# The order of big and small tiles in an expert layer behind an FFT, on one core

## The chip, the core and the metric

The kernel runs on one core of a Trainium2 chip. The metric is device microseconds (us) of one execution. Engines: TensorE (PE, its weight loads PEld), VectorE (DVE), ScalarE (ACT), GpSimd (POOL) and SyncE (SP, which issues most DMA transfers).

## What is computed

```
X = fft(fft(x, axis=1), axis=2).real          # x: 8 x 3072 x 256, so 24576 rows of 256
h = X @ w_in;  g = h * clip(h + 3, 0, 6) / 6;  y = g @ w_out         # first MoE, d_ff 2048
e = argmax(y @ w_gate);  p = softmax(y @ w_gate)[e]                  # 8 experts
out[row] = p * (relu(y @ w1[e]) @ w2[e])                             # second MoE, d_ff 1024
```

## The kernel before

The transform and the first MoE run first, in steps, and scatter each routed row into a region of its expert in DRAM (`xs`). The change does not touch them. Then comes the second MoE, which works in **tiles** of rows of one expert: 41 **big** ones (`NBIG`) of 512 rows, which their experts fill, and 21 **small** ones (`NSMALL`) of 256 rows for what remains; the last three small ones (`SPARE`) run only if the counts need them, and did not here. So 59 tiles run. Tiles 0 and 1 are started early, beside the first MoE. The table of experts and first rows of the others is worked out on the chip in `regs`, big ones first; SP loads an entry of it for each DMA address.

I call the position of a tile in the order of work its **place**, 0 to 58. For the tile at place `i`, `tile_of(i)` writes down:

- `first(i)`: for each of 8 blocks `f` of d_ff, 6 matmuls into one of four PSUM banks (`hp`); ACT takes the high part out (`WA`, relu), DVE the low part (`WB`, a scalar_tensor_tensor, "the low part of hidden block f" below). A bank is free again when DVE has done its low part.
- `prep_w(i + 1)` and `prep_x(i + 1)`: the next tile's weights and rows are split into high and low parts. For weights ACT copies the high part and POOL subtracts (`w1` in two halves, `w2` in two pieces); `prep_w`'s argument sends the first half of `w1` to DVE in some cases. For rows there are, in this order: ACT and DVE each put one 16-bit half of each word into `xf` (ACT an activation, DVE a COPY), ACT copies the high part `xT`, DVE subtracts (`xT <- xf, xT`, "the x subtract" below), and DVE makes the places for the output scatter (`dst`; a CAST for a big tile, two operations on `inv` for a small one).
- `load_x(i + 2)` and `load_w(i + 2)`: DMA from SP's queue, two places ahead. The weights of a tile are 2 MB whatever its rows.
- `second(i)`: for each 128 rows, 24 matmuls (three for each block f, the third of them with the low part) into `op`; DVE scales into `yo`, POOL scatters to `out`.

Buffers alternate with the place: an odd place works from `TB`, `W2a`/`SC`, `xTb`, and during it the next place's `xTa` is made; an even place works from `W1b`, `W2b`, `xTa`, and `xTb` is made. A scheduler fixes the order on each engine before the run, and each engine then takes its instructions strictly in that order, so an instruction is often ahead of where the text has it: `w2` of place i + 1 is split at the start of place i, and `w1` of place i + 2 in the middle of it.

Of the kernel before, what the change touches and what calls it, by code (L numbers as in the profile page):

```python
# [17 lines left out]
ALU = mybir.AluOpType  # L18
AX = mybir.AxisListType
PSUM = bass.MemoryType.PSUM  # L20
SP_ONLY = [mybir.EngineType.SP]

P = 128
# [4 lines left out]
XW = 260  # L28
# rows of a big tile, which its expert fills, and of a small one, which takes what remains
TBIG, TS = 512, 256  # L30
CAPR = NTOK + TS
NBIG = -(-(NTOK - NE * (TBIG - 1)) // TBIG)
NSMALL = (NTOK - NBIG * TBIG + NE * (TS - 1)) // TS
# the tiles that start before the first MoE ends, of the expert with the most rows by then
NEARLY = 2
# [5 lines left out]
SPARE = 3  # L41
# [22 lines left out]
HW = 3 * 4 * 129  # L64
# kind, parity, first column, range of d
X_SEG = ((0, 0, X_T0, 0, 129), (0, 1, X_T1, 1, 128), (1, 0, X_T2, 0, 129), (2, 1, X_T2 + 128, 1, 128),
         (2, 0, X_T3, 0, 129), (1, 1, X_T3 + 128, 1, 128))

# The transform over the sequence splits by s = 1024 a + 3 b (mod 3072) into one over a (3 points) and one
# over b (1024 points) without factors between them; the one over d is merged into w_in. A row k and its  # L70
# mirror -k share the parts P (even in d) and Q (odd in d): h_k = A - B, h_-k = A + B, with A = P W', B = Q W'.


@with_exitstack
def tile_fft_moe(ctx, tc, xr, xf, xcoef, w_in, w_out, w_gate, w1, w2, tabs, fm, misc, tri, sgn8, dstc, maskc, out):
# [16 lines left out]
    est = pa.tile([P, NE], F32, name="est")  # L92
    # what the second MoE uses again
    WA = [pa.tile([P, DFF], F32R, name=f"WA{i}") for i in range(2)]
    WB = [pa.tile([P, DFF], F32R, name=f"WB{i}") for i in range(2)]
    TB = pa.tile([P, 2, 2, TW], F32R, name="TB")
    SC1 = pa.tile([P, 2, 2, 2, 256], F32R, name="SC1")
    # places that hold one tile after another: SS0, SS1, HH0, HH1, RR, pq (two)
    pr = ctx.enter_context(tc.tile_pool(name="pr", bufs=1))
# [54 lines left out]

    # a bank of PSUM for small things
    def bank(name):
# [31 lines left out]

    # ---------------------------------------------------------------- folds of x
    def fold_quarter(R, H, hf, e1, e2):  # L190
# [12 lines left out]

    # kind 0 first: the group g = 0 needs no other
    def fold_whole(H):
# [20 lines left out]

    # closures for one batch: loads and folds of the two half tiles in order, and the splits of each half tile
    def fold_ops(b, e1, e2, rtiles=None):
# [21 lines left out]

    # ---------------------------------------------------------------- transform over b
    PASS = ((0, 0), (0, 1), (1, 0))
# [74 lines left out]

    # the part of d = 128, row 0 of Q, on all partitions
    def fft_bc(b, g, pq):
# [10 lines left out]

    # a group's transform: list of (mm, ev) pieces, and its tiles
    def fft_group(b, g):
# [4 lines left out]

    # ---------------------------------------------------------------- start: constants
    def load_consts():
# [29 lines left out]

    # the folds of the rows b = 256 and 768, which the halves leave out, for all batches: [kind, parity, columns, place]  # L380
    def start_x256():
# [17 lines left out]

    # float64 comes as int64. Times 2^-112, its high word, read as float32, leaves 5 bits of exponent, so that a shift  # L400
    # by 3 makes room for the next bits of the fraction and gives float32; what float32 can't hold goes to 0
    def conv(raw, hi, lo):
# [33 lines left out]

    # w_in's chunk of two blocks of columns: to parts in a half of SC1, which the stacks fill later; then times the transform
    def w_in_conv(c):
# [25 lines left out]

    # logits straight from g: w_out times w_gate beside w_out
    def w_out_mm(c):
# [13 lines left out]

    # ---------------------------------------------------------------- first MoE
    def mm1(ab, f0, pq, c0):
# [16 lines left out]

    # one tile for the rows k of a step, one for their mirrors  # L500
    def halves(tag, dt, s):
# [28 lines left out]

    # a row's high halves of its words, then its low halves
    def halve(xo, xp):
# [4 lines left out]

    # routing of nt token tiles, first of number t0; closures in stages
    def routing(xo, xp, t0, nt, mask, tagn, wait=RKW):
# [64 lines left out]
    if True:  # L604
# [91 lines left out]

        # the folds of batch b + 1 beside batch b, on steps without transforms and ranks
        def plan_folds(b):
# [34 lines left out]

        # the rows of k = 1536 of each batch
        def plan_extra(base):
# [61 lines left out]

        # ------------------------------------------------------------ second MoE: its tiles
        T = {}
# [11 lines left out]

        # what the second early tile waits for
        def second_set():
# [3 lines left out]
        hh = [[W.rearrange("p (f n) -> p f n", n=TBIG) for W in Ws] for Ws in (WA, WB)]  # L817

        def rows(i):
            return TBIG if i < NBIG else TS  # L820

# [9 lines left out]
        def load_x(i):  # L831
            t = T[i] = {}
            n = rows(i)
            v = er[0:1, i:i + 1] if i < NEARLY else regs[0:1, 0, i - NEARLY:i - NEARLY + 1]
            r = ds(reg(v, NE * CAPR - n), n)
            t["gd"] = pk.tile([P, 4, 2], F32, tag="gd", name=f"gd{i}")[:, 0:n // P]
            sp.dma_start(t["gd"], xs.bitcast(F32)[r, D:D + 2].rearrange("(t p) c -> p t c", p=P))
            for w in range(2):
                for k in range(2):
                    c = w * D + k * P  # L840
                    sp.dma_start(xset(i)["x"][:, w, k, 0:n], xs16[r, c:c + P], transpose=True)

        def load_w(i):
            s = kset(i)
            e = reg(er[0:1, 2:3] if i < NEARLY else regs[0:1, 1, i - NEARLY:i - NEARLY + 1], NE - 1)
            sp.dma_start(s["w1"], w1[ds(e, 1)].rearrange("e (k p) f -> p (e k) f", p=P))
            for f0, f1, t in s["w2"]:
                sp.dma_start(t.rearrange("p (f d) -> p f d", d=D),
                             w2[ds(e, 1), f0 * P:f1 * P].rearrange("e (k p) d -> p (e k) d", p=P))

        # closures: the parts of a tile's weights
        def prep_w(i, eng):
# [11 lines left out]
        def prep_x(i):  # L864
            t, v = T[i], xset(i)
            n = rows(i)
            nt = n // P
            xf, t["xT"] = v["xf"][:, :, 0:n], [z[:, :, 0:n] for z in v["xT"]]
            h = xf.bitcast(U16).rearrange("p k (n w) -> p k n w", w=2)
            keep = tc.keep_in_program_order  # L870
            keep(act.activation(h[:, :, :, 1], v["x"][:, 0, :, 0:n], AF.Copy))
            keep(dve.tensor_copy(h[:, :, :, 0], v["x"][:, 1, :, 0:n]))
            act.activation(t["xT"][0], xf, AF.Copy)
            sub(dve, t["xT"][1], xf, t["xT"][0])
            t["dst"] = pk.tile([P, 4], I32, tag="dst", name=f"dst{i}")[:, 0:nt]
            if i < NBIG:
                keep(dve.tensor_copy(t["dst"], t["gd"][:, :, 1]))
            else:
                inv = pk.tile([P, 2], F32, tag="inv", name=f"inv{i}")
                keep(dve.tensor_scalar(inv, iot, vld[:, i - NBIG:i - NBIG + 1], BIG, op0=ALU.is_lt, op1=ALU.mult))  # L880
                keep(dve.tensor_tensor(out=t["dst"], in0=inv, in1=t["gd"][:, :, 1], op=ALU.add))

        # the early tiles' expert and places, from the counts so far
        def early_mm():
# [108 lines left out]

        # ------------------------------------------------------------ the list of tiles
        cps = bank("cps")
# [14 lines left out]

        # per tile: its expert, and its number among the expert's
        def spread(i0, n):
# [16 lines left out]
        dve.tensor_tensor(out=nf[:, 1:NE], in0=cum[:, 1:NE], in1=cum[:, 0:NE - 1], op=ALU.subtract)  # L1029
        # per tile: the sum over its expert of what v holds per expert  # L1030
        def pick(r, v, o, sh):
# [28 lines left out]

        # ------------------------------------------------------------ second MoE
        pd = ctx.enter_context(tc.tile_pool(name="pd", bufs=1, reuse_waits="tile"))
# [21 lines left out]
        def tile_of(i):  # L1084
            if i:
                first(i)
            if i + 1 < last and i:
                if i + 1 >= NEARLY:
                    for f in prep_w(i + 1, lambda n: pool if n or i + 1 < NBIG else dve):
                        f()  # L1090
                prep_x(i + 1)
            if i and i + 2 < last:
                load_x(i + 2)
                load_w(i + 2)
            second(i)
# [19 lines left out]

# [1 line left out]
def _round12(a):  # L1117
# [73 lines left out]

# how the 12 parts (a, row, side) of a batch go into each segment, for its row of high and its row of low parts
def _xcoef():
# [69 lines left out]
```

## Time and profile before

| what | us |
|---|---|
| median of 3 runs (3367.33 to 3371.47) | 3368.87 |
| span of the profiled execution | 3376.2 |
| PE busy in that span | 3082.8 (91%) |
| DVE busy | 2691.3 (80%) |
| POOL busy | 2296.7 (68%) |
| ACT busy | 1809.4 (54%) |
| second MoE from the first matmul of place 1 to the end of the span | 1189.0 |

The page gives no other duration for the profiled execution than its span, which is 7.3 us (0.2%) longer than the median of the timed runs. Shares are means over the whole span; the second MoE is its last third.

### The profile page before, as it was taken

What the parts mean: (1) busy time and instruction counts of PE and PEld (TensorE: products, weight loads), DVE (VectorE), ACT (ScalarE), POOL (GpSimd) and SP (SyncE); (2) the same over time, 40 slices, a digit from 0 to 9 for tenths busy, and PEclk for the clock granted to TensorE, in tenths of its full rate; (3) what the DMA queues carried; (4) which work ended last, traced back from release to release, by engine and by line L of the source; (5) the groups of instructions that cost most, each with busy time, mean ns of one, the idle gap of its engine ahead of it and who ended that gap; (6) DMA issues with size and microseconds to landing.
All of it is one profiled execution on the core that took longest, in us unless ns stands there. A gap on an engine that the chain in (4) does not pass through costs nothing.

```text
span 3376.2 us, 61155 instructions
## 1 busy us (share of the span) xinstructions
PE 3082.8 (91%) x22698; PEld 2948.4 (87%) x22698; DVE 2691.3 (80%) x4453; ACT 1809.4 (54%) x2971; POOL 2296.7 (68%) x1780
## 2 busy tenths in 40 slices
PE   6888889889899989989989999999999999999887
PEld 5888889888899888888988999888899899988787
DVE  8999999999999999999999998845455444546775
ACT  4555555556555555556556665545444544444553
POOL 5576776876866876876876665576666666665654
PEclk8999999999999999999999999999999999999998
DMA  5100100100100100100000001174544454444562
GB/s 188 42 34 23 42 23 14 39 23 14 42 25 14 42 25 14 42 25 14 33 15 15 14 14 51 44 196 140 150 135 137 141 150 133 136 143 133 171 166 74
DMA packets 246975, 242.79 MB, mean 72 GB/s; under 512 B 148523, under 2 KB 209804, under 8 KB 246672
## 3 DMA queue, kind: packets, MB, share of 16 engines
q1 hardware_dynamic: 225424, 184.35, 18.9%
q0 software_dynamic: 21248, 54.48, 4.4%
q8 instruction: 181, 2.97, 0.4%
q14 instruction: 122, 1.00, 0.1%
HBM read 159.71 MB, written 54.04 MB: 63 GB/s over the span
## 4 chain that ended last, share of the span: by engine, by line
PE 45%; DVE 40%; issue 6%; ACT 5%; POOL 2%; DMA 1%; SPq 0%; ACTq 0%; DVEq 0%; POOLq 0%
PE op L163 16%; DVE r L505 15%; PE hp L163 14%; PE acc L510 7%; DVE S L187 7%; PE ab L163 6%; DVE h L182 4%; DVE h L179 4%; ACT r L498 2%; POOL gl L182 1%; DVE H L179 1%; DVE SC L176 1%; DVE H L187 1%; DVE R L179 1%; ACT gh L944 1%
## 5 line engine op out<-in xcount | busy, mean ns | idle before, releaser
L182 POOL TENSOR_TENSOR gl<-r,gh 128x512 fp32r<-128x512 f32 x768 | 1134.3, 1500 | 491.1 <-ACT gh L944 271.4
L510 PE MATMUL acc<-WO,gh 128*128 128x264 f32 x6144 | 844.5, 291 | 15.0 <-ACT xo L529 12.6
L510 PEld LDWEIGHTS acc<-WO,gh 128*128 128x128 f32 x6144 | 805.8, 196 | 16.7 <-ACT xo L529 13.0
L944 ACT ACTIVATE gh<-r 128x512 fp32r<-128x512 f32 x768 | 474.7, 630 | 573.5 <-DVE r L505 437.5
L505 DVE SCALAR_TENSOR_TENSOR r<-r,h 128x512 f32<-128x512 f32 x768 | 733.7, 980 | 36.9 <-ACT r L498 35.8
L498 ACT ACTIVATE r<-h,half 128x512 f32<-128x512 f32 x768 | 523.3, 720 | 236.2 <-DVE h L182 170.7
L163 PE MATMUL ab<-pq,WA 128*128 128x256 f32 x2304 | 425.7, 295 | 155.9 <-DVE rt_mc L548 67.3
L978 DVE SCALAR_TENSOR_TENSOR WB<-hp,WA 128x512 fp32r<-128x512 f32 (+1 forms) x472 | 280.8, 607 | 296.5 <-ACT WA L977 291.0
L163 PEld LDWEIGHTS ab<-pq,WA 128*128 128x128 f32 x2304 | 343.2, 197 | 168.7 <-issue 142.3
L510 PE MATMUL acc<-WO,gl 128*128 128x264 f32 x3072 | 441.2, 285 | 4.8 <-POOL gl L182 4.6
L163 PE MATMUL ab<-pq,WB 128*128 128x256 f32 x2304 | 419.7, 292 | 0.0
L510 PEld LDWEIGHTS acc<-WO,gl 128*128 128x128 f32 x3072 | 402.6, 189 | 7.3 <-POOL gl L182 7.3
L187 DVE SCALAR_TENSOR_TENSOR S<-pb,w,ab 128x256 f32<-128x256 f32 x768 | 334.7, 471 | 55.1 <-PE ab L163 53.5
L977 ACT ACTIVATE WA<-hp 128x512 fp32r<-128x512 f32 (+1 forms) x472 | 245.1, 528 | 214.8 <-PE hp L163 210.0
L163 PEld LDWEIGHTS ab<-pq,WB 128*128 128x128 f32 x2304 | 346.5, 199 | 0.0
L147 POOL DMA_INDIRECT out_dram<-yo,dst x200 | 228.3, 1141 | 147.8 <-DVE yo L1078 121.1
L163 PE MATMUL hp<-xTa,W1b 128*128 128x512 f32 (+1 forms) x1392 | 284.7, 362 | 22.5 <-DVE WB L978 22.5
L163 PEld LDWEIGHTS hp<-xTa,W1b 128*128 128x128 f32 x1392 | 232.4, 189 | 67.4 <-DVE WB L978 25.0
L163 PE MATMUL hp<-xTb,TB 128*128 128x512 f32 (+1 forms) x1344 | 273.9, 363 | 14.8 <-DVE WB L978 14.8
L163 PE MATMUL op<-W2b,WA 128*128 128x256 f32 x1568 | 286.4, 285 | 0.0
L163 PEld LDWEIGHTS hp<-xTb,TB 128*128 128x128 f32 x1344 | 225.6, 192 | 55.8 <-DVE WB L978 16.1
L147 POOL DMA_INDIRECT xs_dram<-xp,pic x192 | 211.3, 1100 | 84.1 <-issue 36.9
(267 smaller groups left out, 5174.8 us busy)
## 6 DMA issues: line engine op xcount, KB each, us to landing
w1a<-in_w_dram SPq DMA_DIRECT2D x29, 1024.0 KB, 5.6
w1b<-in_w_dram SPq DMA_DIRECT2D x29, 1024.0 KB, 5.6
w2b<-in_w_dram SPq DMA_DIRECT2D x58, 512.0 KB, 3.4
R<-in_xr_dram SPq DMA_DIRECT2D x32, 774.0 KB, 4.1
w2a<-in_w_dram SPq DMA_DIRECT2D x29, 768.0 KB, 4.8
w2d<-in_w_dram SPq DMA_DIRECT2D x28, 256.0 KB, 4.3
raw<-in_w_in_dram SPq DMA_DIRECT2D x8, 512.0 KB, 3.8
rawo<-in_w_out_dram SPq DMA_DIRECT2D x8, 512.0 KB, 3.3
```

Of the source, the lines that this page charges most:

```text
L147: i = pool.indirect_dma_start(oob_is_err=False, **kw)
L163: pe.matmul(dst, l, r, start=(n == 0), stop=(n == len(terms) - 1))
L176: pinned(dve.scalar_tensor_tensor(out=lo, in0=src, scalar=scale, in1=hi, op0=ALU.mult, op1=ALU.subtract))
L179: pinned(eng.tensor_tensor(out=o, in0=a, in1=b, op=ALU.add))
L182: i = eng.tensor_tensor(out=o, in0=a, in1=b, op=ALU.subtract)
L187: pinned(dve.scalar_tensor_tensor(out=o, in0=a, scalar=s, in1=b, op0=ALU.mult, op1=ALU.add))
L498: act.activation(r, h, AF.Relu, bias=half, scale=1.0 / 6.0)
L505: dve.scalar_tensor_tensor(out=g, in0=r, scalar=1.0, in1=h, op0=ALU.min, op1=ALU.mult)
L510: pe.matmul(acc[t][:, 0:GW], lhs, wo(w, f0 + i), start=st, stop=sp_)
L944: act.activation(gh[n], g[n], AF.Copy)
L977: act.activation(hi, ps, AF.Relu)
L978: dve.scalar_tensor_tensor(out=lo, in0=ps, scalar=0.0, in1=hi, op0=ALU.max, op1=ALU.subtract)
```

## The change

Before, place and tile number are the same: big tiles at places 0 to 40, small ones at 41 to 58. The change adds a list `order` from place to tile: after the two early tiles come two or three big tiles to each small one, so that the 18 small ones that run stand at places 4, 7, 10, 13, 16, 20, 23, 26, 29, 32, 35, 39, 42, 45, 48, 51, 54 and 58. `rows`, the table lookups and the test for a small tile go through the list. In `tile_of` the rule for the first half of `w1` changes: it goes to DVE when the *current* tile is small, where it went to DVE when the *next* one was small. Buffers, sizes and the number of tiles stay. The rest of the diff deletes comments.

```
+        order = list(range(NEARLY))
+        nb, ns = NBIG - NEARLY, NSMALL - SPARE
+        for n in range(ns):
+            order += range(NEARLY + n * nb // ns, NEARLY + (n + 1) * nb // ns)
+            order.append(NBIG + n)
+        order += range(NBIG + ns, NBIG + NSMALL)
+
         def rows(i):
-            return TBIG if i < NBIG else TS
+            return TBIG if order[i] < NBIG else TS
...
-            v = er[0:1, i:i + 1] if i < NEARLY else regs[0:1, 0, i - NEARLY:i - NEARLY + 1]
+            o = order[i] - NEARLY
+            v = er[0:1, i:i + 1] if i < NEARLY else regs[0:1, 0, o:o + 1]
...
-            if i < NBIG:
+            if order[i] < NBIG:
                 keep(dve.tensor_copy(t["dst"], t["gd"][:, :, 1]))
...
-                    for f in prep_w(i + 1, lambda n: pool if n or i + 1 < NBIG else dve):
+                    for f in prep_w(i + 1, lambda n: pool if n or rows(i) == TBIG else dve):
```

How instructions move is seen at three places. Names carry a running number at their end; line numbers of the changed kernel are 10 higher (L978 has become L988, L182 is the same helper), and `hp_0` to `hp_7` are a tile's eight hidden blocks.

On DVE, within the first products of a small tile at an odd place; before, place 41:

```order
L978 SCALAR_TENSOR_TENSOR WB_71<-hp_0_36603,WA_69 128x256
L978 SCALAR_TENSOR_TENSOR WB_71<-hp_1_36612,WA_69 128x256
L182 TENSOR_TENSOR xTa_26321<-xfa,xTa_26320 128x2x256
L978 SCALAR_TENSOR_TENSOR WB_71<-hp_2_36621,WA_69 128x256
L978 SCALAR_TENSOR_TENSOR WB_71<-hp_3_36630,WA_69 128x256
L978 SCALAR_TENSOR_TENSOR WB_72<-hp_4_36639,WA_70 128x256
```

and after, place 23:

```order
L988 SCALAR_TENSOR_TENSOR WB_71<-hp_0_32343,WA_69 128x256
L988 SCALAR_TENSOR_TENSOR WB_71<-hp_1_32352,WA_69 128x256
L988 SCALAR_TENSOR_TENSOR WB_71<-hp_2_32361,WA_69 128x256
L182 TENSOR_TENSOR xTa_26321<-xfa,xTa_26320 128x1024
L988 SCALAR_TENSOR_TENSOR WB_71<-hp_3_32370,WA_69 128x256
L988 SCALAR_TENSOR_TENSOR WB_72<-hp_4_32379,WA_70 128x256
```

The x subtract has twice the columns, since the next tile is big, and stands one block later.

On DVE, within the first products of a small tile at an even place; before, place 42:

```order
L978 SCALAR_TENSOR_TENSOR WB_71<-hp_2_36783,WA_69 128x256
L182 TENSOR_TENSOR xTb_27748<-xfb,xTb_27747 128x2x256
L978 SCALAR_TENSOR_TENSOR WB_71<-hp_3_36792,WA_69 128x256
L978 SCALAR_TENSOR_TENSOR WB_72<-hp_4_36801,WA_70 128x256
L880 TENSOR_SCALAR inv_36850<-iot,vld 128x2
L978 SCALAR_TENSOR_TENSOR WB_72<-hp_5_36810,WA_70 128x256
L881 TENSOR_TENSOR dst_36849<-inv_36850,gd_36694 128x2
L978 SCALAR_TENSOR_TENSOR WB_72<-hp_6_36819,WA_70 128x256
L182 TENSOR_TENSOR W1b_27742<-w1b,W1b_27741 128x1024
L978 SCALAR_TENSOR_TENSOR WB_72<-hp_7_36828,WA_70 128x256
L872 COPY xfa<-xa 128x2x256
```

and after, place 20:

```order
L988 SCALAR_TENSOR_TENSOR WB_71<-hp_3_31772,WA_69 128x256
L182 TENSOR_TENSOR xTb_27748<-xfb,xTb_27747 128x1024
L988 SCALAR_TENSOR_TENSOR WB_72<-hp_4_31781,WA_70 128x256
L988 SCALAR_TENSOR_TENSOR WB_72<-hp_5_31790,WA_70 128x256
L988 SCALAR_TENSOR_TENSOR WB_72<-hp_6_31799,WA_70 128x256
L887 CAST dst_31829<-gd_31616 128x4
L988 SCALAR_TENSOR_TENSOR WB_72<-hp_7_31808,WA_70 128x256
L1088 TENSOR_SCALAR yo_31846<-op_0_31847,gd_31396 128x256
```

The x subtract now stands behind the fourth low part, the half of `W1b` and the COPY are gone from here, and a CAST stands ahead of the last low part.

On POOL, in the same two tiles; before, place 42:

```order
L147 DMA out_dram<-yo_36706,dst_36467 24576x256 x2
L182 TENSOR_TENSOR SC_74<-w2a,W2a_26317 128x1536
L182 TENSOR_TENSOR SC_74<-w2d,W2a_26317 128x512
L182 TENSOR_TENSOR W1b_27742<-w1b,W1b_27741 128x1024
L147 DMA out_dram<-yo_36868,dst_36687 24576x256
```

and after, place 20:

```order
L147 DMA out_dram<-yo_31628,dst_31391 24576x256 x4
L182 TENSOR_TENSOR SC_74<-w2a,W2a_26317 128x1536
L182 TENSOR_TENSOR SC_74<-w2d,W2a_26317 128x512
L182 TENSOR_TENSOR W1b_27742<-w1b,W1b_27741 128x1024 x2
L147 DMA out_dram<-yo_31846,dst_31609 24576x256
L182 TENSOR_TENSOR W2b_27744<-w2b,W2b_27743 128x1024
L147 DMA out_dram<-yo_31846,dst_31609 24576x256
```

Both halves of `W1b` are POOL's in a small tile now; the half that DVE does has moved into the big tile ahead of it.

## Rows read from the trace of the kernel before

**Rows 1.** Windows (length, engines' busy us, PEclk, DMA share, GB/s): places 1-39, 41-57, 58.

```profile
2187.20:3069.40 882.20, 880.31 (x5618) 794.11 (x5617) 444.32 (x597) 421.09 (x549) 582.37 (x316) 1.00 0.51 147
...
3093.10:3352.40 259.30, 215.83 (x1635) 212.16 (x1634) 185.32 (x253) 128.50 (x235) 153.91 (x84) 0.92 0.51 148
3352.40:3376.20 23.80, 11.47 (x97) 11.26 (x96) 4.85 (x11) 3.09 (x8) 2.92 (x3) 0.81 0.06 19
```

**Rows 2.** Windows of one small tile each: places 41, 42 and 57.

```profile
3093.10:3108.70 15.60, 13.14 (x98) 12.93 (x97) 11.17 (x15) 7.08 (x14) 9.13 (x5) 0.89 0.35 108
3108.70:3122.90 14.20, 11.74 (x99) 11.53 (x98) 11.23 (x15) 8.28 (x15) 8.41 (x5) 1.00 0.55 164
...
3336.90:3352.40 15.50, 13.07 (x99) 12.87 (x98) 7.74 (x13) 4.85 (x11) 6.78 (x4) 0.89 0.06 22
```

**Rows 3.** Waits from 3093.1 to 3352.4: total, times, longest (us).

```profile
PE hp L163 <- DVE WB L978: 34.7, 14, 2.6
...
PE op L163 <- DVE WB L978: 8.8, 3, 2.9
```

**Rows 4.** Groups by form, 3093.1 to 3352.4: busy us, mean ns, idle before.

```profile
L978 DVE SCALAR_TENSOR_TENSOR WB<-hp,WA 128x256 fp32r<-128x256 f32 x136 | 53.9, 416 | 29.6 <-ACT WA L977 26.1 <-ACT W2a L859 3.5
L182 DVE TENSOR_TENSOR xTb<-xfb,xTb 128x512 fp32r<-128x512 f32 x8 | 29.4, 3672 | 0.8
...
L182 POOL TENSOR_TENSOR W1b<-w1b,W1b 128x1024 fp32r<-128x1024 f32 x8 | 19.1, 2391 | 31.0 <-ACT W1b L859 31.0
...
L859 ACT ACTIVATE W1b<-w1b 128x1024 fp32r<-128x1024 f32 x16 | 16.9, 1054 | 21.1 <-PE hp L163 21.1
```

**Rows 5.** Timeline, place 41 (from 3093.1): start, us, engine, instruction [idle before].

```profile
3094.57 0.79 ACT L871 ACTIVATE xfa<-xa 128x512 uint16<-128x512 uint16 x1
...
3096.13 3.45 DVE L182 TENSOR_TENSOR xTa<-xfa,xTa 128x512 fp32r<-128x512 f32 x1
3099.51 0.74 DVE L978 SCALAR_TENSOR_TENSOR WB<-hp,WA 128x256 fp32r<-128x256 f32 x2
...
3096.65 2.38 POOL L182 TENSOR_TENSOR W2b<-w2b,W2b 128x1024 fp32r<-128x1024 f32 x1
...
3099.97 0.39 PE L163 MATMUL hp<-xTb,TB 128*128 128x256 f32 x1 [2.46 <-DVE WB L978]
```

**Rows 6.** Timeline, place 42 (from 3108.7).

```profile
3109.64 0.61 ACT L859 ACTIVATE W2a<-w2d 128x512 fp32r<-128x512 f32 x1
...
3110.66 3.52 POOL L182 TENSOR_TENSOR SC<-w2a,W2a 128x1536 fp32r<-128x1536 f32 x1
3114.12 1.28 POOL L182 TENSOR_TENSOR SC<-w2d,W2a 128x512 fp32r<-128x512 f32 x1
...
3112.26 3.70 DVE L182 TENSOR_TENSOR xTb<-xfb,xTb 128x512 fp32r<-128x512 f32 x1
...
3116.34 0.86 PE L163 MATMUL hp<-xTa,W1b 128*128 128x256 f32 x5 [2.46 <-DVE WB L978]
```

**Rows 7.** Timeline, big tiles at places 35 (from 2956.6) and 36.

```profile
2968.31 5.30 POOL L182 TENSOR_TENSOR TB<-w1a,TB 128x1024 fp32r<-128x1024 f32 x2 [5.70 <-ACT TB L859]
...
2969.36 2.02 DVE L872 COPY xfa<-xa 128x1024 uint16<-128x1024 uint16 x1
...
2971.47 1.06 ACT L873 ACTIVATE xTa<-xfa 128x1024 fp32r<-128x1024 f32 x1 [1.81 <-DVE xfa L872]
...
2972.57 2.13 DVE L182 TENSOR_TENSOR xTa<-xfa,xTa 128x1024 fp32r<-128x1024 f32 x1 [0.82 <-ACT xTa L873]
...
2980.60 1.36 ACT L871 ACTIVATE xfb<-xb 128x1024 uint16<-128x1024 uint16 x1
```

**Rows 8.** Timeline near 2142, beside the first MoE.

```profile
2142.85 1.25 DVE L877 CAST dst<-gd 128x4 int32<-128x4 f32 x1
...
2138.84 6.49 POOL L182 TENSOR_TENSOR gl<-r,gh 128x512 fp32r<-128x512 f32 x4
```

**Rows 9.** Timeline, PE at place 40, the last big tile.

```profile
3077.38 2.84 PE L163 MATMUL hp<-xTa,W1b 128*128 128x512 f32 x11 [0.78 <-DVE WB L978]
```

More of the change, by code (lines that the diff above doesn't have):

```diff
@@ L844, in load_w @@
             s = kset(i)
-            e = reg(er[0:1, 2:3] if i < NEARLY else regs[0:1, 1, i - NEARLY:i - NEARLY + 1], NE - 1)
+            o = order[i] - NEARLY
+            e = reg(er[0:1, 2:3] if i < NEARLY else regs[0:1, 1, o:o + 1], NE - 1)
             sp.dma_start(s["w1"], w1[ds(e, 1)].rearrange("e (k p) f -> p (e k) f", p=P))
@@ L879, in prep_x @@
                 inv = pk.tile([P, 2], F32, tag="inv", name=f"inv{i}")
-                keep(dve.tensor_scalar(inv, iot, vld[:, i - NBIG:i - NBIG + 1], BIG, op0=ALU.is_lt, op1=ALU.mult))
+                keep(dve.tensor_scalar(inv, iot, vld[:, order[i] - NBIG:order[i] - NBIG + 1], BIG, op0=ALU.is_lt, op1=ALU.mult))
                 keep(dve.tensor_tensor(out=t["dst"], in0=inv, in1=t["gd"][:, :, 1], op=ALU.add))
```

## The prediction

> **What bounds the kernel now.** I read the windows first, cut at the first matmul of a place. Places 1 to 39, all big, take 882.2 us with PE busy for 880.3 at a granted clock of 1.00 [rows 1]: 22.62 us each, and nothing on another engine or a queue shows. In units of 256 columns a big tile is 192 matmuls, so one takes 0.118 us, a hidden block of a small tile (6 of them) 0.707, its first product 5.65 and the whole small tile 11.31. The 17 small tiles at places 41 to 57 take 259.3 us, 15.25 each: 3.94 more than PE needs, 67.0 us in all. That is the most that the change can win.
>
> Next I asked what PE waits for there: 17 waits of 43.5 us together, all for a low part on DVE [rows 3]. The rest is mostly clock. Place 42 takes 14.2 us at 1.00, place 41 takes 15.6 at a mean of 0.89 [rows 2], so part of it ran at the lower level, 1.2 GHz of 2.4, and that costs 1.4 us; 11 of the 17 windows, the first and the last among them, are under 1.00.
>
> Why is DVE late? At place 41 the x subtract starts at 3096.13 and takes 3.45 us, while POOL subtracts `W2b` from 3096.65 to 3099.03 [rows 5]; it ends 0.55 after POOL does. At place 42 it waits likewise for two subtracts of POOL, `SC` from `w2a` and from `w2d`, to 3115.40, and ends at 3115.96 [rows 6]. So it can't run beside a POOL subtract. The low parts queued behind it come late, and so do the PSUM banks: at place 41 block 6 is due 4.24 us into the tile and starts at 6.87; at place 42 block 7 is due at 4.95 and starts at 7.64. Delays of 2.6 and 2.7; with some 0.2 to fill the pipeline this gives 11.31 + 2.69 + 0.2 = 14.2, as measured.
>
> **What moves.** A small tile's two neighbours are now big. Averages would say that its weights, x and DMA then have 22.6 us of cover, and DVE, ACT and POOL are all less than full there. But the question is what stands in the 11.3 us of the small tile itself, in order. I take the times of the rows and put the new order under them; t is the time from the tile's first matmul.
>
> *Odd places, eight small tiles (7 to 51).* POOL's second `W2b` subtract keeps its place, t = 3.55 to 5.93 [rows 5]: a big tile ahead is followed by the same scatter, as at place 41. ACT's first x half starts at 1.47 [rows 5], takes 1.36 for 1024 columns in place of 0.79, then come two high parts and the copy of 1.06 [rows 7], so the x subtract is ready at 4.4, after POOL has begun. It ends 1.09 behind POOL's end (2974.70 against 2973.61 for the same form in a big tile [rows 7]): at 7.02. Behind it stands the fourth low part, 0.42 [rows 4], done at 7.4; block 7 needs its bank at 4.95. Delay 2.5, hardly less than now. A tile takes 11.31 + 2.5 + 0.2 = 14.0, and with the lower clock as often as now (11/17 of 1.4 = 0.9) 14.9; eight take 119.3.
>
> *Even places, nine small tiles (4 to 54).* ACT is free of `W2a` at 1.55 [rows 6]; two high parts, the x half (1.36), two high parts and the copy (1.06) make the x subtract ready at 4.9. Four low parts stand ahead of it, done by 4.4, so no bank is late. POOL is in its `SC` pair until t = 6.70 [rows 6], the subtract ends at 7.79 and the fifth low part at 8.2. The second product, from 5.65, needs it for its 15th matmul at 7.30: 0.9 late. Then comes a new collision. POOL now does both halves of `W1b` here, the first when ACT has copied it (6.6, from 1.05 behind block 7's third matmul) and the port is free: 7.75 to 10.2 at 2.39 to 2.45 each [rows 4, 7]. DVE comes to the CAST at 8.7. A CAST of the same 4 columns took 1.25 us beside POOL's subtracts [rows 8], so it too waits; here until 10.2. The last low part, behind it, is done at 10.65, and the 24th matmul wanted it at 8.36: delay 2.3 in all, the 0.9 included. That is 13.8 us a tile. The stall is in two parts of 0.9 and 1.4 with matmuls between, so I give it half the clock loss, 0.45: 14.25, and 128.3 for nine.
>
> *The rest.* The 17 take 247.6 in place of 259.3: 11.7 less. Place 40 loses its wait of 0.8 [rows 9]. Place 58 is small and last as before, without an x subtract ahead of it. The DVE half of `w1` (1.2 us) stands in the big tile ahead of a small one, between its last two low parts; a big tile has four banks of 1.41 us ahead and its second product wants the last low part only 2.6 us after it starts, so I cost this at nothing; with a stall of 1 us at each of 17 it would take the gain back. SP's queue has the same loads, two places ahead, behind the same releases; DMA is busy for 0.51 in both stretches [rows 1], no PE wait ends at a transfer, and a tile ahead of or behind a small one has more time than small ones have now. Sum: 12.5 us less, 3363.7 for the profiled span of 3376.2, which is 7.3 over the median; from the median, **3356**.
>
> **A rule weighed.** The subtract at place 42 was issued before POOL's second `SC` subtract began and still let it pass: it ends 0.56 behind that one [rows 6], and the eight of this kind in the stretch take 3.67 on average [rows 4]. At place 35 the COPY that came during POOL's first `TB` subtract ended at 2971.38, before the second one did at 2973.61 [rows 7]. So the port goes over between two POOL instructions in one case and not in the other. The Trainium skill, "SBUF — State Buffer", section "Who interferes with whom", says that of a DVE operation with two SBUF inputs and a GpSimd operation reading SBUF the one that issues first holds the shared port for its whole instruction. By that the subtract would go ahead of the second `SC`; it is the second rival below, and the eight rows speak against it for this pair.
>
> **Rivals.**
> - *Slower: POOL keeps the port in even small tiles.* As with the `SC` pair, the x subtract lets the first half of `W1b` pass too, which then runs 6.7 to 9.1. The subtract ends at 10.2, POOL's second half runs to 12.6, the CAST behind it, and the last low part is done at 13.1 against 8.36: 4.75 late, 17.2 us a tile with the clock, nine 154.4. The 17 then take 273.7, which is 14.4 more, less 0.8 for place 40: **3382**. It turns the sign when the even delay passes 3.3. For it: the `SC` pair. Against: `W1b`'s copy by ACT ends at 6.6, 0.1 before the port is free, so POOL is hardly waiting there yet.
> - *The port goes over between the `SC` subtracts.* The x subtract ends at 6.6, all low parts are in time, the CAST passes between two of POOL's. Even tiles take 11.5, the 17 take 222.9: **3332**.
> - *Full cover.* Odd tiles don't stall either: 17 x 11.5 = 195.5, **3304**. Only if the odd x subtract were ready before t = 3.55; rows put it 0.9 later.
> - *No change: the clock falls at every stall.* 15.4 x 8 + 15.2 x 9 = 260.0, **3369**. For it: 11 of 17 now. Against: six delays of the same size left it at 1.00.
>
> **How the numbers follow.** Forecast 0.48, its own range 3348 to 3366 (the clock lost at fewer or more of the stalls, 6 either way). Slower 0.15, the port passed over 0.16, full cover 0.04, no change 0.13, anything else 0.04. The range 3328 to 3374 leaves out full cover and slower, 0.19. A difference under 0.2%, 6.7 us, can't be told from none here. Faster by more: 0.41 of the forecast's 0.48, 0.16, 0.04 and 0.01, together 0.62. Within: 0.07, 0.13 and 0.02, together 0.22. Slower: 0.16.
>
> **What would show it.** Big tiles still at 22.6 us. In odd small tiles PE waits near t = 5 for about 2.5 us, and the x subtract ends 1.1 behind POOL's `W2b`. In even ones no wait in the first product, two in the second, the CAST takes some 1.5 us and the x subtract 2.9. Even tiles of 11.5 us mean that the port went over within the `SC` pair, of 17 us that POOL kept it. The forecast is wrong if big tiles beside small ones stall, or if a load comes late: then ACT's copy of `w1` or `w2` would be waited for with nothing on an engine ahead of it.

## The result and the profile after

The changed kernel takes 3342.87 us (median of 4 runs, 3341.19 to 3344.07); the kernel before, run beside it, takes 3370.17. The ratio is 0.9911, 95% interval 0.9896 to 0.9927, so 25 to 35 us faster. The forecast was 12.5 us, to 3356: right in sign, less than half in size, and the time is 5 us below the forecast's own range (3348 to 3366). The profiled execution has a span of 3341.6 us.

The page, first the busy time of each engine, then the granted clock of TensorE in 40 slices:

```profile
PE 3068.6 (92%) x22698; PEld 2934.2 (88%) x22698; DVE 2642.0 (79%) x4452; ACT 1805.6 (54%) x2971; POOL 2285.8 (68%) x1781
...
PEclk9999999999999999999999999999999999999999
```

The windows, in the columns of [rows 1]: a big tile, then the small tiles at places 26 (even), 29 (odd) and 32 (even):

```profile
2639.80:2662.40 22.60, 22.60 (x146) 20.38 (x145) 11.24 (x15) 11.26 (x15) 16.31 (x10) 1.00 0.61 173
...
2685.00:2698.50 13.50, 11.89 (x99) 11.48 (x98) 8.05 (x12) 8.84 (x15) 12.39 (x6) 1.00 0.61 179
2743.60:2757.00 13.40, 11.72 (x98) 11.43 (x97) 6.70 (x12) 7.91 (x14) 10.00 (x5) 1.00 0.59 181
2802.20:2817.20 15.00, 13.40 (x98) 13.00 (x97) 8.03 (x12) 8.87 (x15) 12.96 (x7) 0.89 0.69 180
```

Big tiles are as before. Of the 17 small tiles (places 4 to 54) only place 32 is under a clock of 1.00; before, by the windows of all 17, of which [rows 2] shows three, 12 were (the prediction counted 11). From first matmul to first matmul the 17 take 230.6 us, where they took 259.3: 28.7 less. Over places 3 to 57, with place 40's wait gone too, it is 29.8. The two profiled executions differ by 34.6; 4.6 of the rest lie ahead of place 0, which starts at 2158.4 here and at 2163.0 before, and no edit reaches there.

PE's waits from place 4 on (total, times, longest) answer to [rows 3]:

```profile
PE op L163 <- DVE WB L988: 14.4, 18, 0.9
PE hp L163 <- DVE WB L988: 13.5, 8, 1.7
```

The even tiles wait 18 times in the second product, twice each, the odd ones once each in the first, 1.69 us in place of 2.5. So 27.9 us of waiting is left of 43.5, 15.6 less. The other 13 are the clock: eleven tiles fewer at the lower one, at about 1.5 us each, would be 16, and by an estimate from the tiles at 1.00 some 3 are lost again, since a tile loses 0.3 us (before) to 0.6 us (even tiles now, with two waits) beyond its waits. The timeline of place 26 (t = 0 at 2685.0) shows the even tile:

```profile
2686.93 3.54 POOL L182 TENSOR_TENSOR SC<-w2a,W2a 128x1536 fp32r<-128x1536 f32 x1
...
2689.82 2.98 DVE L182 TENSOR_TENSOR xTb<-xfb,xTb 128x1024 fp32r<-128x1024 f32 x1 [0.47 <-ACT xTb L883]
2690.40 1.32 POOL L182 TENSOR_TENSOR SC<-w2d,W2a 128x512 fp32r<-128x512 f32 x1
...
2691.66 5.74 POOL L182 TENSOR_TENSOR W1b<-w1b,W1b 128x1024 fp32r<-128x1024 f32 x2
...
2693.20 0.39 PE L163 MATMUL op<-W2b,WB 128*128 128x256 f32 x1 [0.68 <-DVE WB L988]
...
2693.73 1.34 DVE L887 CAST dst<-gd 128x4 int32<-128x4 f32 x1
...
2695.45 0.38 PE L163 MATMUL op<-W2b,WB 128*128 128x256 f32 x1 [0.92 <-DVE WB L988]
```

The x subtract was there before POOL's second `SC` subtract, lets it pass and ends at 2692.80, t = 7.80 (forecast 7.79). PE waits; then the CAST stands behind POOL's first half of `W1b`, ends at t = 10.07 (forecast 10.2), and PE waits for the last low part. Place 29 (t = 0 at 2743.6) shows the odd tile:

```profile
2747.19 2.41 POOL L182 TENSOR_TENSOR W2b<-w2b,W2b 128x1024 fp32r<-128x1024 f32 x1
...
2747.96 2.72 DVE L182 TENSOR_TENSOR xTa<-xfa,xTa 128x1024 fp32r<-128x1024 f32 x1 [0.46 <-ACT xTa L883]
...
2749.11 0.28 PE L163 MATMUL op<-W2a,WA 128*128 128x256 f32 x1
...
2751.07 0.98 PE L163 MATMUL hp<-xTb,TB 128*128 128x256 f32 x6 [1.68 <-DVE WB L988]
```

The x subtract ends at t = 7.08 (forecast 7.02) and block 7 starts at 7.47, as forecast. But ahead of block 7 stand four matmuls of the second product, the last at 2749.11: PE's order has changed too, which I had not looked at. PE works 4 x 0.118 = 0.47 us longer before it waits.

### The profile page after: what moved, and what is told of

Same layout as the page of the kernel before. It is cut to its first block, busy times and chain, and to the rows that moved or that the text cites. A ratio compares the mean times of both kernels' runs of the same rounds, so it can differ in the third digit from the quotient of the medians.

```text
span 3341.6 us, 61178 instructions
## 1 busy us (share of the span) xinstructions
PE 3068.6 (92%) x22698; PEld 2934.2 (88%) x22698; DVE 2642.0 (79%) x4452; ACT 1805.6 (54%) x2971; POOL 2285.8 (68%) x1781
## 3 DMA queue, kind: packets, MB, share of 16 engines
q1 hardware_dynamic: 225424, 184.35, 19.8%
## 4 chain that ended last, share of the span: by engine, by line
PE 47%; DVE 40%; ACT 5%; issue 4%; POOL 2%; DMA 1%; SPq 0%; ACTq 0%; DVEq 0%; POOLq 0%
PE op L163 16%; PE hp L163 15%; DVE r L505 15%; PE acc L510 8%; DVE S L187 7%; PE ab L163 6%; DVE h L182 4%; DVE h L179 3%; ACT r L498 2%; POOL gl L182 1%; DVE H L187 1%; DVE H L179 1%; DVE SC L176 1%; DMA raw<-in_w_in_dram 1%; DVE R L179 1%
## 5 line engine op out<-in xcount | busy, mean ns | idle before, releaser
L182 POOL TENSOR_TENSOR gl<-r,gh 128x512 fp32r<-128x512 f32 x768 | 1128.8, 1493 | 488.7 <-ACT gh L954 255.5
L988 DVE SCALAR_TENSOR_TENSOR WB<-hp,WA 128x512 fp32r<-128x512 f32 (+1 forms) x472 | 278.8, 607 | 299.2 <-ACT WA L987 299.1
L147 POOL DMA_INDIRECT out_dram<-yo,dst x200 | 217.5, 1088 | 155.5 <-DVE yo L1088 117.6
L163 PE MATMUL hp<-xTb,TB 128*128 128x512 f32 (+1 forms) x1344 | 277.3, 364 | 13.5 <-DVE WB L988 13.5
L163 PE MATMUL hp<-xTa,W1b 128*128 128x512 f32 (+1 forms) x1392 | 275.5, 357 | 1.5 <-DVE WB L988 1.5
L163 PE MATMUL op<-W2b,WA 128*128 128x256 f32 x1536 | 276.5, 282 | 0.0
L1088 DVE TENSOR_SCALAR yo<-op,gd 128x256 f32<-128x256 f32 x200 | 95.4, 478 | 218.0 <-PE op L163 218.0
```

The source lines that it names most:

```text
L147: i = pool.indirect_dma_start(oob_is_err=False, **kw)
L163: pe.matmul(dst, l, r, start=(n == 0), stop=(n == len(terms) - 1))
L182: i = eng.tensor_tensor(out=o, in0=a, in1=b, op=ALU.subtract)
L988: dve.scalar_tensor_tensor(out=lo, in0=ps, scalar=0.0, in1=hi, op0=ALU.max, op1=ALU.subtract)
L1088: dve.tensor_scalar(yo[:, j], ps[:, 0:D], t["gd"][:, j, 0:1], None, op0=ALU.mult)
```

## The experiments

Times are medians; each ratio is to the kernel before on the same chip. The first MoE, which no edit touches, ends sooner or later from execution to execution: place 0 starts between 2145 and 2163 us in the traces. So small effects are read from the tiles' own times, which I sum for the 17 small tiles (the last tile not counted). The expectations give some waits 0.16 to 0.18 us longer than the rows do (1.86 for 1.68, 0.85 and 1.08 for 0.68 and 0.92, 2.31 for 2.15); the text goes by the rows.

**The order of PE in odd tiles** (`e1_pe_order`): the first matmul of each second product is pinned on PE behind block 7. The order of the other engines stays as in the changed kernel.

```
-   mm_group(ps[:, 0:D], [...])
+   for m, (f, (a, c)) in enumerate((f, ac) for f in range(8) for ac in PASS):
+       o = pe.matmul(ps[:, 0:D], ..., start=m == 0, stop=m == 23)
+       if i >= NEARLY and not j and not m:
+           tc.keep_in_program_order(o)
```

> The changed kernel with one thing undone: in a small tile TensorE's queue has the first product's last block (hp_7) ahead of the second product again, as in the kernel before; in the changed kernel four matmuls of the second product stand ahead of it in the eight odd small tiles. Those tiles took 13.45 us after the change, with a wait of 1.86 us. Theory A (a single wait of some 2.5 us lets the granted clock fall, shorter or divided ones don't): the odd tiles' wait is 2.5 us again, 13.45 + 0.6 = 14.05 us each, and most of them (11 of 17 before) lose a further 1.5 us to the lower clock: 8 x 0.6 + 5 x 1.5 = +12, about 3355 us. Theory B (small tiles keep the clock because each stands among big ones without a wait, whatever the wait's length): only the 0.6 us each, +5, about 3348 us, and granted clock 1.00 in all odd tiles. The even small tiles stay at 13.5 us in both.

Measured: 3351.55 us, ratio 0.9942 (0.9928 to 0.9956). The waits, the window of place 29, and its wait on PE:

```profile
PE hp L163 <- DVE WB L988: 17.2, 8, 2.2
...
2744.60:2760.00 15.40, 13.25 (x98) 12.96 (x97) 6.68 (x12) 7.85 (x14) 11.55 (x6) 0.89 0.54 158
...
2752.13 0.97 PE L163 MATMUL hp<-xTb,TB 128*128 128x256 f32 x6 [2.15 <-DVE WB L988]
```

With 0.47 us less cover the wait is 2.15 us, and all eight odd tiles, among big ones as they are, fall to 0.89: 15.43 us in place of 13.45. Theory B, that big neighbours keep the clock, falls. The 17 small tiles take 246.6 us, 16 more; 12 of these are clock, for 4 of waiting. This is 1.0 off the 247.6 that I had forecast.

**Rule and order apart** (`e2_rule_only`, the first pair of lines, on the kernel before; `e3_order_only`, the second, on the changed one):

```
-   for f in prep_w(i + 1, lambda n: pool if n or i + 1 < NBIG else dve):
+   for f in prep_w(i + 1, lambda n: pool if n or i < NBIG else dve):
...
-   for f in prep_w(i + 1, lambda n: pool if n or rows(i) == TBIG else dve):
+   for f in prep_w(i + 1, lambda n: pool if n or rows(i + 1) == TBIG else dve):
```

> The kernel before with the rule for the first half of W1b in its new form (VectorE while the tile at hand is small) and the order left as it was. Only the preparation of place 40, which falls into the last big tile, goes from VectorE to GpSimd. If the order is the whole change, the time is that of the kernel before, 3369 us within 3 us, with 11 or so of the 17 small tiles at the lower clock. If the rule is what brought the time down, it is faster by more than 5 us.

> The changed kernel with the old rule for the first half of W1b (VectorE if the tile prepared is small, otherwise GpSimd). The instructions then stand otherwise on VectorE: in a small tile all eight low parts come ahead of the copy and the x subtract of the next tile, which the changed kernel has after the third or fourth low part; GpSimd's two W1b halves for a big tile lie in the small tile in both. Theory A (the x subtract, which takes turns with GpSimd's subtracts, is all that delays the low parts): no wait is left in the small tiles, 11.4 us each in place of 13.5, 17 x 2.1 = -36 us, about 3307 us. Theory B (the order is what pays, and the rule is needed with it): the next big tile gets its x or its weights late and waits for them, so the 2 us come back there: 3340 to 3350 us.

Measured: the rule alone 3368.33 us, 0.9992 (0.9983 to 1.0), which is no change, with 12 of 17 small tiles at the lower clock. The order alone 3336.01 us, 0.9904 (0.9889 to 0.9918), as much as the whole change. The mechanism is theory B's. The median is 4 us below its range, but the tiles take no less than in the changed kernel, as the sums below show; in the profiled executions the difference lies ahead of place 0, which starts at 2145 here, at 2158 in the changed kernel. Its waits, and a small tile with the big one behind it:

```profile
PE hp L163 <- DVE xTb L182: 12.1, 9, 1.3
PE hp L163 <- DVE xTa L182: 10.1, 8, 1.3
PE hp L163 <- DVE WB L988: 6.3, 8, 0.8
...
2672.50:2683.80 11.30, 11.30 (x98) 11.30 (x97) 6.77 (x12) 8.57 (x15) 10.30 (x5) 1.00 0.47 101
2683.80:2708.00 24.20, 22.85 (x147) 20.38 (x146) 14.42 (x19) 10.85 (x15) 13.66 (x9) 1.00 0.71 180
```

No small tile waits. With the old rule the COPY of the next big tile's x stands behind the last low part, not in the big tile ahead, so its x subtract comes late and the next big tile starts 1.3 us late for `xT`. The small tiles fall to 194.1 us and the 38 big ones from place 3 on rise from 857.6 to 895.2: 1089.3 together, against 1088.1 of the changed kernel. So the new rule moves the wait from the big tiles into the small ones; it neither wins nor loses.

**The x subtract last** (`e4_x_last`; `hold["lo"]` is the tile's latest low part):

```
+   o = sub(dve, t["xT"][1], xf, t["xT"][0])
+   if i > NEARLY and rows(i - 1) == TS:
+       tc.add_manual_dep(o.ins, hold["lo"].ins.name, <order on the engine only>)
```

> The changed kernel with one thing more: while a small tile runs, the x subtract of the next tile (and the CAST behind it) stands on VectorE behind the last low part. Theory A (x subtract between the low parts is the only cause of the small tiles' waits): 17 small tiles at about 11.4 us in place of 13.5, -36 us, about 3307 us, and granted clock 1.00 there. Theory B (GpSimd's W1b, which the x subtract lets pass, and ScalarE's copies are late as well, or x comes too late for the next tile): the wait moves to the start of the next big tile, and 10 us or less is gained, 3333 us or more.

Measured: 3303.75 us, 0.9804 (0.9791 to 0.9817). This beats the kernel before by 66 us and the changed one by 36 by the ratios (39 by the medians). PE has no wait for another engine from place 4 to the last tile. A small tile, and the big one behind it:

```profile
2666.70:2678.10 11.40, 11.40 (x99) 11.40 (x98) 7.39 (x11) 9.00 (x15) 10.21 (x5) 1.00 0.80 199
...
2678.10:2700.60 22.50, 22.50 (x146) 20.31 (x146) 12.86 (x17) 10.12 (x15) 17.13 (x10) 1.00 0.66 185
```

Theory A holds: the small tiles take 194.7 us, 36 less, and the next tile gets its x in time.

**The same edit in the order of before** (`e5_before_x_last`):

> The kernel before, with its order and its rule, and one thing more: while a small tile runs, the x subtract of the next tile (and what follows it for dst) stands on VectorE behind the last low part, as in e4_x_last. Theory A (the place of the x subtract is the cause, and mixing the tiles is only another way to thin it out): the 17 small tiles in a row fall from 15.25 us on the mean to about 11.4, -65 us, some 3304 us, as fast as e4_x_last. Theory B (small tiles in a row are also held by GpSimd, which has some 9.2 us of subtracts and scatters in each, or by their loads): 12.5 us or more each, or the clock still falls, 3323 us or more, and the mixing is worth 20 us of its own.

Measured: 3315.56 us, 0.9833 (0.9819 to 0.9848), between the theories. Its waits, the window of the small tiles (places 41 to 57), and an operation of place 46:

```profile
PE op L163 <- DVE WB L981: 8.0, 15, 0.6
...
3087.30:3292.40 205.10, 197.07 (x1635) 194.01 (x1634) 151.53 (x253) 126.75 (x235) 165.10 (x84) 1.00 0.66 187
...
3153.90 2.14 DVE L182 TENSOR_TENSOR W1b<-w1b,W1b 128x1024 fp32r<-128x1024 f32 x1 [0.52 <-ACT W1b L859]
```

The clock is whole, and a wait of 0.5 to 0.6 us is left in 15 tiles: the last low part stands behind DVE's half of the next `w1`, as at place 46 behind that of `W1b`, 2.14 us beside POOL. So without any mixing this edit, which leaves the order of the tiles alone, brings 259.3 us down to 205; with the change it is 194.7. The change by itself is worth 10 us once the cause is gone.

**Small tiles in pairs** (`e6_pairs`):

```
-   for n in range(ns):
-       order += range(NEARLY + n * nb // ns, NEARLY + (n + 1) * nb // ns)
-       order.append(NBIG + n)
+   for n in range(0, ns, 2):
+       order += range(NEARLY + n * nb // ns, NEARLY + (n + 2) * nb // ns)
+       order += [NBIG + n, NBIG + n + 1]
```

> The changed kernel with two small tiles together after every four or five big ones, in place of one after every two or three: eight pairs and a single one. The first of a pair has a small tile next, as in the kernel before; the second has a big one next, as in the changed kernel. Theory A (what counts is what a small tile prepares, and whether its wait is one long one): the eight first ones cost what they cost before, 14 to 15.6 us with a wait of 2.3 to 2.6 us and mostly a lower clock, the nine others 13.5: about 8 x 1.5 = +12, 3355 us. Theory B (standing among big tiles is what keeps the clock): no tile but a few at the lower clock, 3345 us or less.

Measured: 3357.93 us, 0.996 (0.9947 to 0.9974), as theory A has it. Nine tiles have a small one next: six of them are at the lower clock, three keep 1.00 with the same wait. The first rows are the first and the second of a pair; the third and fourth are the second of another (place 13):

```profile
2292.80:2308.40 15.60, 13.15 (x98) 12.95 (x97) 11.49 (x15) 8.19 (x15) 9.12 (x6) 0.89 0.84 184
2308.40:2321.90 13.50, 11.82 (x99) 11.55 (x98) 6.70 (x12) 8.08 (x14) 10.17 (x5) 1.00 0.63 172
...
2427.80:2441.50 13.70, 11.74 (x98) 11.42 (x98) 6.96 (x12) 8.15 (x15) 10.19 (x5) 1.00 0.67 177
...
2435.45 0.98 PE L163 MATMUL hp<-xTb,TB 128*128 128x256 f32 x6 [1.96 <-DVE WB L988]
...
2573.25 8.02 DVE L182 TENSOR_TENSOR xTb<-xfb,xTb 128x1024 fp32r<-128x1024 f32 x1 [0.47 <-ACT xTb L883]
...
2574.29 1.31 POOL L182 TENSOR_TENSOR SC<-w2d,W2a 128x512 fp32r<-128x512 f32 x1
2575.53 4.65 POOL L182 TENSOR_TENSOR W1b<-w1b,W1b 128x1024 fp32r<-128x1024 f32 x2
...
3077.62 3.94 DVE L182 TENSOR_TENSOR xTa<-xfa,xTa 128x1024 fp32r<-128x1024 f32 x1 [0.46 <-ACT xTa L883]
```

The next three rows are from one even tile (place 20) in which the slower rival of the prediction came true: the x subtract let the second `SC` and both halves of `W1b` pass, 8.02 us, and that tile took 19.8 us. It is the only even tile of all runs with such a subtract. ACT's copy of `W1b` ended 0.6 us before POOL's second `SC` subtract there, 0.2 before it in the changed kernel, where the x subtract came next nine times of nine. The last row is from an odd tile (place 45) that theory A did not foresee either: POOL's second `W2b` starts 0.47 us behind the x subtract there and goes ahead of it, PE waits for 2.91 us, and the tile takes 16.2 us at 0.89. In this trace the 17 small tiles take 253.1 us, 22.6 more than in the changed kernel, and these two make 9 of that.

**The CAST last** (`e7_cast_last`): the pin of `e4_x_last`, on the CAST of `dst` alone.

> The changed kernel with the CAST of dst alone, not the x subtract, put behind the last low part of a small tile. Theory A (the even small tiles' second wait, 1.08 us, is the CAST that stands behind GpSimd's W1b subtract and ahead of the last low part): the nine even ones fall from 13.5 to about 12.4 us, their first wait of 0.85 us stays, the odd ones keep 13.45 us: -9 us, about 3334 us. Theory B (the last low part would itself wait for GpSimd, with or without the CAST ahead of it): no change, 3343 us.

Measured: 3329.84 us, 0.9883 (0.9868 to 0.9897).

```profile
PE hp L163 <- DVE WB L991: 13.6, 8, 1.7
PE op L163 <- DVE WB L991: 6.1, 9, 0.7
```

Nine of the 18 waits in the second product are gone, the others stay: theory A. Even tiles take 12.3 us, and the 17 small ones 218.4.

**Without GpSimd's subtracts** (`e8_no_pool`), which leaves out 119 of them by POOL's count of instructions:

```
+   if eng(n) is pool and i > NEARLY + 2 and TS in (rows(i - 1), rows(i - 2)):
+       return
    sub(eng(n), lo, raw, hi)
```

> The changed kernel without GpSimd's subtracts for the two tiles behind each small one (110 of them; the low parts of those weights are then old ones). VectorE's order stays as in the changed kernel, the x subtract between the low parts included. Theory A (the x subtract is late because it takes turns with GpSimd's subtracts, and takes only about 1.3 us by itself): its 2.5 to 3 us fall to about 1.3, the low parts behind it come in time, the small tiles take 11.4 to 12 us, 3307 to 3317 us. Theory B (a long operation between the low parts delays them even without GpSimd): 12.5 us or more each, 3326 us or more.

Measured: 3308.57 us, 0.9813 (0.9799 to 0.9828). The waits, and an x subtract of an even tile:

```profile
PE hp L163 <- DVE WB L990: 1.5, 8, 0.2
...
2673.42 1.23 DVE L182 TENSOR_TENSOR xTb<-xfb,xTb 128x1024 fp32r<-128x1024 f32 x1 [0.47 <-ACT xTb L885]
```

On the same order of DVE the subtract takes 1.23 us in place of 2.98, and nearly all waiting is gone: the small tiles take 197.4 us. Theory A holds. It is GpSimd beside the x subtract, together with its place ahead of the low parts, that makes PE wait; either taken away is enough.

**One long wait or the sum** (`e9_even_two_waits`): after `e1_pe_order` I held that a single long wait makes the clock fall and that divided ones don't.

```
+   for _ in range(3 if rows(i) == TS and i % 2 == 0 and f == 7 else 1):
        dve.scalar_tensor_tensor(out=lo, in0=ps, scalar=0.0, in1=hi, op0=ALU.max, op1=ALU.subtract)
```

> The changed kernel, in whose even small tiles VectorE does the last low part three times in place of once (the same values; 0.42 us each). Their second wait grows from 1.08 to about 1.9 us, the first stays 0.85, so that they wait 2.75 us in all, more than the odd tiles of e1_pe_order do (2.31 us in one wait, at the lower clock 8 times of 8), but in no single wait as long as those. Theory A (the length of the single wait decides): the granted clock stays at 1.00 in nearly all nine, 14.35 us each, 8 us more than the changed kernel, about 3351 us. Theory B (the sum of a tile's waits decides): it falls in most of them, 15.8 us each, 18 to 21 us more, about 3362 us.

Measured: 3360.43 us, 0.9966 (0.9949 to 0.9982): my theory A falls.

```profile
PE op L163 <- DVE WB L989: 22.6, 18, 1.8
PE hp L163 <- DVE WB L989: 13.6, 8, 1.7
...
2694.20:2710.00 15.80, 13.31 (x98) 12.91 (x97) 8.87 (x14) 8.86 (x15) 13.49 (x7) 0.90 0.67 190
2755.20:2768.70 13.50, 11.81 (x98) 11.51 (x98) 6.70 (x12) 7.97 (x14) 10.06 (x5) 1.00 0.60 179
...
2263.10:2265.10 2.00, 1.67 (x8) 1.67 (x9) 0.76 (x2) 0.00 (x0) 1.60 (x2) 0.51 0.17 9
...
2263.43 0.58 PE L163 MATMUL op<-W2b,WB 128*128 128x256 f32 x1 [1.83 <-DVE WB L989]
```

All nine even tiles are at 0.89 to 0.91, though no single wait is longer than 1.84 us; the odd ones with their 1.7 keep 1.00. So dividing a wait does not save the clock, and the longest wait does not decide: place 13 of `e6_pairs` kept 1.00 through a single wait of 1.96 us, and at place 4 here (the last two rows) the clock was down at 2263.10, about 1.5 us into the second wait. The sum of a tile's waits orders these tiles better, though not wholly: single waits of some 2.5 us passed at 1.00 too, before the change and in `e6_pairs`.

## Why the prediction was too small

**What held.** Big tiles at 22.6 us; no load late; the waits of the 17 small tiles in the places and for the operations named; the ends of the x subtracts and of the CAST within 0.15 us of the forecast. The mechanism, VectorE's x subtract behind GpSimd's subtracts with the low parts queued behind it, is shown by `e4_x_last`, `e7_cast_last` and `e8_no_pool`, each of which takes one piece of it away. That the x subtract lets the second `SC` pass but goes ahead of `W1b` came as forecast in nine of nine even tiles. The Trainium skill ("SBUF — State Buffer", section "Who interferes with whom") has it that issue order decides which of the two is blocked. By that the subtract of place 26, which starts at 2689.82, would go ahead of POOL's second `SC`, which starts at 2690.40; the trace does not agree, and the same happens in all nine even tiles.

**Which step failed.** The clock term: "with the lower clock as often as now (11/17 of 1.4 = 0.9)" for odd tiles and "half the clock loss, 0.45" for even ones. It is 9.8 of the 17 us by which the 17 tiles undercut their forecast, 230.6 us in place of 247.6; the other 7.1 are delays that came out shorter:

| term | forecast | measured | difference |
|---|---|---|---|
| odd tiles, clock | 8 x 0.9 | 0 | -7.2 |
| even tiles, clock | 9 x 0.45 | 1 x 1.5 | -2.6 |
| odd tiles, without clock | 8 x 14.0 | 8 x 13.45 | -4.4 |
| even tiles, without clock | 9 x 13.8 | 9 x 13.5 | -2.7 |

In the odd tiles four matmuls of PE shortened the delay (below); in the even ones the last block's matmul starts at t = 10.45, where the forecast had its low part done at 10.65 and added 0.2 to fill the pipeline. The clock terms of the forecast amount to some eight tiles at the lower clock; one was. I carried the present share of slow tiles over to stalls that had become a little shorter. But this share is no constant. PE's waits in a small tile, summed, and the tiles at the lower clock:

| waits, us | where | at the lower clock |
|---|---|---|
| 0.5 to 0.7 | `e5_before_x_last`, even tiles of `e7_cast_last` | 0 of 24 |
| 1.6 to 1.7 | the changed kernel; odd tiles of `e7_cast_last` and `e9_even_two_waits`, even ones of `e1_pe_order`; five tiles of `e6_pairs` with a big one next | 2 of 47 |
| 1.96, in one | place 13 of `e6_pairs` | 0 of 1 |
| 2.15, in one | odd tiles of `e1_pe_order` | 8 of 8 |
| 0.67 + 1.82 | even tiles of `e9_even_two_waits` | 9 of 9 |
| 2.2 to 2.9, in one | the kernel before; `e2_rule_only`; `e6_pairs` with a small one next | 12 of 17; 12 of 17; 6 of 9 |
| 2.9 and 5.7, in one | places 45 and 20 of `e6_pairs` | 2 of 2 |

Between 1.7 and 2.15 us half a microsecond of waiting per tile therefore decides over another 1.5. Nor was the reason for the half in even tiles, that the stall is divided, a good one: `e9_even_two_waits` shows that dividing doesn't help. They kept the clock with two waits that are short together. What lets about a third of the 2.5 us waits pass at 1.00 is not settled, nor why place 32 alone fell in the changed kernel.

**What I overlooked.** The half microsecond in odd tiles came from PE's order, four matmuls ahead of block 7. The prediction took the new order on DVE and POOL and kept PE's of before. Undone in `e1_pe_order`, this gives 246.6 us for the 17 tiles, near the forecast for another reason in part: block 7 starts at t = 7.43, as forecast at 7.4, and each odd tile pays 1.5 of clock where I had 0.9, the even ones less than I had. So 16 of the 29 us that the small tiles gained hang on four matmuls. The prediction also put all waits of before down to the x subtract: at places 43, 45 and 47, the three waits in the second product of [rows 3], that subtract took only 0.7 to 0.8 us, and DVE came late by an `inv` of 2.44 us and its half of `TB`, 3.33 us, both beside POOL's subtracts. And five delays, not six, of about 2.5 us had kept 1.00.

**The rivals.** "Slower" (POOL keeps the port) did not come in the changed kernel, though one tile of `e6_pairs` shows that it can. "The port goes over between the `SC` subtracts", with 3332, is nearer to the measured 3342.87 than the forecast is, but not by what happened: the x subtract in place 26 excludes it. "Full cover" is excluded by the odd tiles' wait of 1.69 us, "no change" by the 16 of 17 stalled tiles that kept 1.00.

## What to carry to other kernels

Look at the order of each engine that is waited for and that waits, the bound one included: four matmuls that the scheduler put ahead of a stalled block were worth more than half the gain. A stall on TensorE had a price in clock here besides its length, and it came steeply: find in the trace at which stalls the granted clock fell and at which it did not, add up those that lie close together, and don't carry a mean share to stalls of another size. And when a long VectorE operation that GpSimd holds up stands ahead of short ones that TensorE waits for, put it behind them first: this one edit won some 36 us more on the changed kernel, and on the order of before alone twice what the change did.

## What was not expected of the hardware

Two waits of 0.67 and 1.82 us, with some 1.3 us of matmuls between, cost the clock as one of 2.15 us did, where one of 1.96 did not. An x subtract of 128x1024 on VectorE took 1.23 us with no GpSimd subtract beside it, mostly 2.7 to 3.0 beside one or two of them, and 8.02 us in the one case in which it ended only behind four of them, run back to back.
